# An RWKV-6 layer followed by a SwiGLU block: the same 1063 steps emitted in another order

## The chip, the cores and the metric

One core of a Trainium2 chip runs one launch of the kernel. The metric is device time in microseconds, the median of several executions. A profile of one execution goes with it; its times count from its own start.

## The reference

```python
# attention: B=4, H=8, S=768, D=48, float32
for t in range(S):
    cur = einsum('bhd,bhe->bhde', u * k[t], v[t])
    y[t] = einsum('bhd,bhde->bhe', r[t], state + cur)
    state = w[t][..., None] * state + einsum('bhd,bhe->bhde', k[t], v[t])
x = y as (B*S, H*D) = (3072, 384)
# feed-forward, d_ff = 1536
xn = x / sqrt(mean(x*x) + 1e-6) * rms_g
out = (silu(xn @ w_gate) * (xn @ w_val)) @ w_out
```

## The kernel before

The sequence is cut into six stages `n` of 128 tokens. A stage does this for its four batch entries `j`, and a step is named `function.n.j`. In the feed-forward part the second number of `gate_mm`, `val_mm`, `silu` and `h_mul` is `f`, one of 12 slices of d_ff, and covers all four batch entries (512 tokens).

The chunked recurrence for one (n, j) is this chain: `load_w` (SP), `ln` (ACT), `cs_mm` (PE: running sums of log w, into a ps_a and, in stages 0 to 2, a ps_b bank; `cs_add` on DVE makes the second one in stages 3 to 5), `exp_r` and `exp_k` (ACT), `r_mul` and `k_mul` (DVE: the scaled r and k, from `load_r` and `load_k`), their transpose, `q_mm` (PE, two ps_q banks), the masks `q_mask_e` (DVE) and `q_copy_o` with `q_mask_o` (ACT, then GpSimd; in stage 0 `q_mask_o` is on DVE and there is no copy), `y_mm` (PE). The transpose is `rk_pe` (PE) and a copy `rk_tr` (ACT) in stages 0 and 1, and a transposing DMA `rk_tr` on SP's queue from stage 2 on. The bonus term goes through `bonus_mul` (GpSimd, two instructions), `bonus_sum` (DVE) and `bonus_v` (GpSimd, from `load_v`). `cast_v` makes v bf16 (ACT in stages 0 and 1, GpSimd later). `st_mm` (PE) and `st_new` (DVE) carry the state to the next stage; `w_tot` (DVE) copies the decay of the chunk.

Then come `x_add` (DVE), `x_sq` (ACT), `x_rstd` (ACT in stage 0, GpSimd later), `xn_mul` (ACT), a transpose (`xn_pe` on PE and `xn_out` on DVE in stages 0 to 3; `xn_tr` by DMA on SP's queue and `xn_gain` on DVE in stages 4 and 5), and the feed-forward part: `gate_mm` (PE, three matmuls of 128x512 into a ps_a bank), `silu` (ACT), `val_mm` (PE, into a ps_b bank), `h_mul` (DVE, into a slice of the tile ht), `o_mm` (PE, 12 matmuls of 128x384, one for each f), `o_out` (ACT or DVE), `out_dma` (SP). The feed-forward of stage n is emitted among the recurrence of stage n+1. In the last stage `o_mm.5.3` and `o_mm.5.4` are the two halves of one batch entry.

The order of work is written out by hand in a string, `ORDER`. Each step is called once in that order:

```python
    for step in ORDER.split():
        fn, n, j = step.split(".")
        fns[fn](int(n), int(j))
```

Every engine runs its own instructions strictly in this order, SP's DMA queue included. What counts is therefore the order of the steps that share an engine. A step that waits holds back all that stand behind it on its engine, not the other engines. Tiles come from pools of fixed size: ps_a and ps_b have two banks each, ps_q four, inputs eight buffers for each of r, k, v and four for pairs of w, silu outputs three. The next allocation waits until a former holder has been read for the last time. The loads of one (n, j) are 192 KB each, with rows of 192 bytes.

The gate and value weights (`load_gv`, in a part for f below 4 and one for the rest) and the output weights (`load_wo`, three parts) go through GpSimd's queue, behind the GpSimd steps that are emitted ahead of them. `ln`, `exp_r`, `exp_k` and stage 0's `x_rstd` use one ACT table set, `silu` another:

```python
    def act(table_name, **kw):
        if table[0] != table_name:
            nc.scalar.preload_act_table_set(table_name)
            table[0] = table_name
        return nc.scalar.activation(**kw).ins
```

Each change between them in emission order loads a table.

Of the kernel before, what the change touches and what calls it, by code (L numbers as in the profile page):

```python
# [25 lines left out]
load_w.0.0 load_v.0.0 load_w.0.1 load_k.0.0 load_r.0.0 ln.0.0 load_w.0.2 load_r.0.1 ln.0.1 cs_mm.0.0 load_k.0.1  # L26
cs_mm.0.1 exp_k.0.0 load_w.0.3 exp_r.0.0 k_mul.0.0 bonus_mul.0.0 exp_r.0.1 r_mul.0.0 exp_k.0.1 load_r.0.2 w_tot.0.0
cast_v.0.0 rk_pe.0.0 ln.0.2 load_k.0.2 st_mm.0.0 r_mul.0.1 rk_tr.0.0 cs_mm.0.2 load_w.1.0 st_new.0.0 bonus_mul.0.1
q_mm.0.0 k_mul.0.1 load_v.0.1 w_tot.0.1 bonus_sum.0.0 ln.0.3 rk_pe.0.1 exp_k.0.2 q_mask_e.0.0 load_k.0.3 exp_r.0.2
cs_mm.0.3 q_mask_o.0.0 bonus_v.0.0 rk_tr.0.1 load_r.0.3 y_mm.0.0 k_mul.0.2 bonus_mul.0.2 exp_k.0.3 q_mm.0.1 load_w.1.1  # L30
r_mul.0.2 exp_r.0.3 x_add.0.0 ln.1.0 rk_pe.0.2 load_v.0.2 bonus_sum.0.1 x_sq.0.0 q_mask_e.0.1 cast_v.0.1 bonus_v.0.1
load_v.0.3 w_tot.0.2 rk_tr.0.2 q_mask_o.0.1 cs_mm.1.0 k_mul.0.3 load_w.1.2 q_mm.0.2 bonus_sum.0.2 bonus_mul.0.3
r_mul.0.3 load_k.1.0 q_mask_o.0.2 ln.1.1 rk_pe.0.3 x_rstd.0.0 load_w.1.3 cast_v.0.2 y_mm.0.1 bonus_v.0.2 rk_tr.0.3
load_r.1.0 x_add.0.1 load_gv.0.0 q_mask_e.0.2 cast_v.0.3 load_r.1.1 xn_mul.0.0 bonus_sum.0.3 load_gv.0.1 q_mm.0.3
ln.1.2 y_mm.0.2 bonus_v.0.3 x_sq.0.1 q_mask_e.0.3 st_mm.0.1 exp_k.1.0 w_tot.0.3 x_add.0.2 load_gv.1.1 cs_mm.1.1
x_rstd.0.1 q_mask_o.0.3 exp_r.1.0 load_gv.1.0 x_sq.0.2 y_mm.0.3 exp_k.1.1 xn_pe.0.0 x_add.0.3 st_mm.0.2 x_rstd.0.2
st_new.0.1 xn_mul.0.1 x_sq.0.3 st_new.0.2 st_mm.0.3 load_v.1.0 cs_mm.1.2 x_rstd.0.3 xn_out.0.0 xn_mul.0.2 xn_pe.0.1
# [643 lines left out]
```

## Time and profile before

| | |
|---|---|
| time, median of 3 runs | 207.25 us (207.13 to 207.8) |
| profiled execution, span from first to last instruction | 206.0 us |
| PE / DVE / ACT / GpSimd busy | 190.5 / 159.0 / 138.4 / 108.4 us |
| DMA | 32.41 MB, 157 GB/s on the mean |
| ACT table loads | 10, of 1283 ns |
| first `gate_mm` starts | 29.28 us |
| `o_mm.0.0` starts | 53.45 us |
| `o_mm.4.0` starts | 172.7 us |

The profiled execution's own time is known only as its span, 206.0 us; the timed median lies 1.25 us above it. The page gives busy time for each engine. PE's busy time has pipelined matmuls in it, so that a stretch can read as full at half the rate of another one; the spacing of the matmuls' starts tells the rate. In rows of the timeline the first number is the start, the second the duration of the row (with "xN", of N instructions together), and brackets give the idle time ahead and what ended it.

### The profile page before, as it was taken

To read this page: it belongs to the slowest core of one execution; us is meant where nothing else is said; L and a number is where in the kernel's file an instruction comes from. 1 tells how busy PE (TensorE), PEld (TensorE's weight loads), DVE (VectorE), ACT (ScalarE), POOL (GpSimd) and SP (SyncE) were. 2 spreads that over 40 slices of the span, in tenths; PEclk is the share of its full clock that TensorE was granted. 3 is DMA by queue.
4 is the path that set the end of the run, shared out by engine and by line. 5 is a ranking of instruction groups with operands and counts; after the bars stand their busy time and mean duration, and the time that the engine had idled before them with its cause. 6 is when DMAs were issued, how large, how long until landed. Compare 5 with 4: busy or idle time off the path is not lost.

```text
span 206.0 us, 4352 instructions
## 1 busy us (share of the span) xinstructions
PE 190.5 (92%) x1507; PEld 111.9 (54%) x1524; DVE 159.0 (77%) x323; ACT 138.4 (67%) x282; POOL 108.4 (53%) x167
## 2 busy tenths in 40 slices
PE   4695869899899999999999999999999999999993
PEld 2353534465665555765556565556555555555563
DVE  6398854799999899999999989899997855146311
ACT  3776994778987646989537978759978962334300
POOL 3398603399679668992699957948505510000000
PEclk9999999999999999999999999999999999999999
DMA  5999999999999899999899889796166110201032
GB/s 118 213 203 201 182 200 202 215 163 222 181 219 215 164 210 230 194 234 201 174 201 223 199 192 203 164 236 144 38 161 199 40 38 3 76 0 40 0 119 76
DMA packets 125727, 32.41 MB, mean 157 GB/s; under 512 B 120580, under 2 KB 124552, under 8 KB 125704
## 3 DMA queue, kind: packets, MB, share of 16 engines
q1 hardware_dynamic: 123664, 28.58, 66.8%
q0 software_dynamic: 2032, 3.54, 9.5%
q8 instruction: 12, 0.20, 0.4%
q14 instruction: 11, 0.09, 0.1%
q10 hardware_dynamic: 8, 0.00, 0.0%
HBM read 25.96 MB, written 4.72 MB: 149 GB/s over the span
## 4 chain that ended last, share of the span: by engine, by line
PE 69%; SPq 18%; DMA 5%; ACT 2%; POOL 2%; issue 1%; DVE 1%; ACTq 0%; DVEq 0%; POOLq 0%
PE ps_q L629 21%; PE ps_a L566 19%; PE ps_b L566 19%; SPq L211 15%; SPq L228 3%; DMA wo_sb<-in_moe_w_out_dram 3%; PE ps_q L458 2%; DMA rt<-in_r_dram 2%; PE ps_q L503 2%; PE ps_q L506 2%; PE ps_a L378 1%; PE ps_q L486 1%; PE ps_q L540 1%; POOL ruk L423 1%; PE ps_a L381 1%
## 5 line engine op out<-in xcount | busy, mean ns | idle before, releaser
L584 DVE TENSOR_TENSOR ht<-ps_b,sg 128x512 bf16<-128x512 f32 x72 | 49.0, 688 | 20.9 <-PE ps_b L566 14.5
L198 ACT ACTIVATE sg<-ps_a 128x512 bf16<-128x512 f32 x72 | 42.9, 598 | 32.6 <-PE ps_a L566 30.6
L566 PE MATMUL ps_a<-xnt,wg_sb 128*128 128x512 bf16 x207 | 59.3, 386 | 1.3 <-DMA wg_sb<-in_moe_w_gate_dram 0.5
L566 PE MATMUL ps_b<-xnt,wv_sb 128*128 128x512 bf16 x208 | 58.6, 384 | 0.3
L629 PE MATMUL ps_q<-wo_sb,ht 128*128 128x384 bf16 (+1 forms) x300 | 50.1, 319 | 0.3 <-DMA wo_sb<-in_moe_w_out_dram 0.3
L629 PEld LDWEIGHTS <-ht 128*128 128x128 bf16 x300 | 27.9, 97 | 16.8 <-DMA wo_sb<-in_moe_w_out_dram 0.5
L423 POOL TENSOR_TENSOR ruk<-rt,kt 128x384 f32<-128x384 f32 x24 | 24.6, 1024 | 22.6 <-DMA rt<-in_r_dram 15.4
L566 PEld LDWEIGHTS <-wv_sb 128*128 128x128 bf16 x216 | 23.6, 115 | 20.8 <-issue 2.1
L566 PEld LDWEIGHTS <-wg_sb 128*128 128x128 bf16 x216 | 23.4, 115 | 20.8 <-issue 1.3
L424 POOL TENSOR_TENSOR ruk<-ruk,u_bc 128x384 f32<-128x384 f32 x24 | 23.9, 997 | 1.9
L476 POOL TENSOR_SCALAR_AFFINE_SELECT qts<-qts 128x512 bf16<-128x512 bf16 x20 | 13.0, 650 | 14.4 <-ACT qts L469 14.4
L433 POOL TENSOR_TENSOR ydiag<-vt,diag 128x384 f32<-128x384 f32 x24 | 19.8, 830 | 0.0
L465 DVE TENSOR_TENSOR qts<-ps_q,mask_lt 128x512 bf16<-128x512 f32 x24 | 16.4, 683 | 2.1 <-PE ps_q L460 1.7
L529 ACT ACTIVATE xn<-xb,rstd 128x384 bf16<-128x384 f32 x24 | 14.4, 608 | 2.0 <-POOL rstd L525 1.9
L198 ACT ACTIVATE lw<-wt 128x384 bf16<-128x384 f32 x24 | 12.1, 516 | 4.8 <-DMA wt<-in_w_dram 4.6
L511 DVE TENSOR_TENSOR xb<-ps_q,ydiag 128x384 f32<-128x384 f32 x24 | 13.2, 551 | 2.0 <-PE ps_q L506 1.9
L469 ACT CAST qts<-ps_q 128x512 bf16<-128x512 f32 x20 | 11.6, 582 | 4.5 <-PE ps_q L460 4.5
L196 ACT ACT_TABLE_LOAD x10 | 12.8, 1283 | 1.8 <-PEq L665 1.6
L636 DVE COPY ob<-ps_q 128x384 f32<-128x384 f32 (+1 forms) x13 | 7.0, 539 | 8.7 <-PE ps_q L629 8.7
L516 ACT ACTIVATE junk<-xb 128x384 bf16<-128x384 f32 x24 | 12.5, 519 | 1.9 <-DVE xb L511 1.5
L428 DVE TENSOR_REDUCE diag<-ruk 128x8 f32<-128x384 f32 x24 | 12.9, 544 | 0.0
L417 DVE TENSOR_TENSOR rk<-kt,ps_b 128x384 bf16<-128x384 f32 x20 | 11.0, 548 | 2.4 <-DMA kt<-in_k_dram 1.9
(71 smaller groups left out, 269.6 us busy)
## 6 DMA issues: line engine op xcount, KB each, us to landing
wt<-in_w_dram SPq DMA_DIRECT2D x24, 192.0 KB, 3.9
vt<-in_v_dram SPq DMA_DIRECT2D x24, 192.0 KB, 3.8
kt<-in_k_dram SPq DMA_DIRECT2D x24, 192.0 KB, 3.8
rt<-in_r_dram SPq DMA_DIRECT2D x24, 192.0 KB, 3.9
out_dram<-ob SPq DMA_DIRECT2D x23, 192.0 KB, 2.2
wo_sb<-in_moe_w_out_dram POOLq DMA_DIRECT2D x3, 384.0 KB, 6.3
wv_sb<-in_moe_w_val_dram POOLq DMA_DIRECT2D x1, 768.0 KB, 10.7
wg_sb<-in_moe_w_gate_dram POOLq DMA_DIRECT2D x1, 768.0 KB, 14.2
```

Source lines behind the costliest of these rows:

```text
L198: return nc.scalar.activation(**kw).ins
L211: dmas["load_" + which, n, j] = nc.sync.dma_start(out=inp[which, n, j], in_=t[j, :, n * L:(n + 1) * L, :].rearrange("h t d -> t h d")).ins
L423: nc.gpsimd.tensor_tensor(out=ruk[n, j], in0=inp["r", n, j], in1=inp["k", n, j], op=ALU.mult)
L424: nc.gpsimd.tensor_tensor(out=ruk[n, j], in0=ruk[n, j], in1=u_bc, op=ALU.mult)
L433: nc.gpsimd.tensor_tensor(out=ydiag[n, j], in0=inp["v", n, j], in1=diag[n, j].to_broadcast([128, H, D]), op=ALU.mult)
L465: nc.vector.tensor_tensor(out=qts[n, j][:, 0], in0=bank["q", n, j][0], in1=bc_mid(mask_lt, NP), op=ALU.mult)
L476: nc.gpsimd.affine_select(out=qts[n, j][:, 1], in_=qts[n, j][:, 1], compare_op=ALU.is_gt, fill=0.0, base=0, pattern=[[0, NP], [1, 128]], c ...
L511: nc.vector.tensor_tensor(out=xb[n, j], in0=bank.pop(("y", n, j)), in1=ydiag[n, j].rearrange("p h d -> p (h d)"), op=ALU.add)
L529: nc.scalar.activation(out=xn, in_=xb[n, j], func=AF.Copy, scale=rstd[n, j][:, 1:2])
L566: nc.tensor.matmul(ps, lhsT=units(ws, c, f), rhs=xnt[n][:, c, :], start=(c == 0), stop=(c == KC - 1))
L584: nc.vector.tensor_tensor(out=ht[n][:, f, :], in0=bank.pop(("v", n, f)), in1=bank.pop(("sg", n, f)), op=ALU.mult)
L629: nc.tensor.matmul(ps[:, cols], lhsT=ht[n][:, f, b * L:(b + 1) * L], rhs=wo_sb[:, f, cols], start=(f == 0), stop=(f == FC - 1))
```

## The change

The string `ORDER` is replaced. It holds the same 1063 steps, each once; no function and no constant changes. The steps keep their engines. All six stages are reordered, the f slices of the feed-forward among them. The places that the prediction speaks of:

```diff
 ORDER = """
-load_w.0.0 load_v.0.0 load_w.0.1 load_k.0.0 load_r.0.0 ln.0.0 load_w.0.2 load_r.0.1 ln.0.1 cs_mm.0.0 load_k.0.1
-cs_mm.0.1 exp_k.0.0 load_w.0.3 exp_r.0.0 k_mul.0.0 bonus_mul.0.0 exp_r.0.1 r_mul.0.0 exp_k.0.1 load_r.0.2 w_tot.0.0
-cast_v.0.0 rk_pe.0.0 ln.0.2 load_k.0.2 st_mm.0.0 r_mul.0.1 rk_tr.0.0 cs_mm.0.2 load_w.1.0 st_new.0.0 bonus_mul.0.1
-q_mm.0.0 k_mul.0.1 load_v.0.1 w_tot.0.1 bonus_sum.0.0 ln.0.3 rk_pe.0.1 exp_k.0.2 q_mask_e.0.0 load_k.0.3 exp_r.0.2
...
-x_rstd.0.1 q_mask_o.0.3 exp_r.1.0 load_gv.1.0 x_sq.0.2 y_mm.0.3 exp_k.1.1 xn_pe.0.0 x_add.0.3 st_mm.0.2 x_rstd.0.2
-st_new.0.1 xn_mul.0.1 x_sq.0.3 st_new.0.2 st_mm.0.3 load_v.1.0 cs_mm.1.2 x_rstd.0.3 xn_out.0.0 xn_mul.0.2 xn_pe.0.1
-xn_mul.0.3 xn_out.0.1 xn_pe.0.2 ln.1.3 xn_pe.0.3 xn_out.0.2 exp_r.1.1 xn_out.0.3 exp_k.1.2 cs_mm.1.3 k_mul.1.0
-exp_r.1.2 gate_mm.0.0 st_new.0.3 exp_k.1.3 exp_r.1.3 val_mm.0.0 silu.0.0 gate_mm.0.1 h_mul.0.0 val_mm.0.1 silu.0.1
...
+load_w.0.0 load_w.0.1 load_r.0.1 load_r.0.0 ln.0.1 cs_mm.0.1 exp_r.0.1 ln.0.0 cs_mm.0.0 exp_r.0.0 r_mul.0.0 load_k.0.0
+bonus_mul.0.0 exp_k.0.0 k_mul.0.0 w_tot.0.0 load_w.0.2 rk_pe.0.0 r_mul.0.1 rk_tr.0.0 q_mm.0.0 load_w.0.3 load_k.0.1
+bonus_mul.0.1 bonus_sum.0.0 w_tot.0.1 exp_k.0.1 ln.0.2 k_mul.0.1 q_mask_o.0.0 cs_mm.0.2 load_v.0.0 ln.0.3 load_k.0.2
+q_mask_e.0.0 exp_k.0.2 k_mul.0.2 cs_mm.0.3 cast_v.0.0 rk_pe.0.1 exp_r.0.2 load_r.0.2 r_mul.0.2 load_v.0.1 bonus_v.0.0
+y_mm.0.0 rk_pe.0.2 rk_tr.0.1 q_mm.0.1 q_mask_e.0.1 q_mask_o.0.1 exp_r.0.3 load_r.0.3 load_w.1.0 cast_v.0.1 ln.1.0
+rk_tr.0.2 bonus_mul.0.2 bonus_sum.0.2 w_tot.0.2 load_v.0.2 cast_v.0.2 load_v.1.0 cast_v.1.0 load_w.1.3 bonus_sum.0.1
+bonus_v.0.1 w_tot.0.3 x_add.0.0 exp_k.0.3 x_sq.0.0 bonus_v.0.2 q_mm.0.2 y_mm.0.1 x_add.0.1 r_mul.0.3 x_sq.0.1
+x_rstd.0.1 load_k.0.3 k_mul.0.3 bonus_mul.0.3 st_mm.0.0 rk_pe.0.3 q_mask_e.0.2 cs_mm.1.0 st_mm.0.2 q_mask_o.0.2
+x_rstd.0.0 xn_mul.0.1 ln.1.3 bonus_sum.0.3 st_new.0.0 rk_tr.0.3 load_gv.0.0 load_gv.0.1 load_k.1.0 load_w.1.1
+load_v.0.3 bonus_v.0.3 cast_v.0.3 exp_k.1.0 y_mm.0.2 x_add.0.2 x_sq.0.2 xn_mul.0.0 x_rstd.0.2 load_w.1.2 ln.1.2
+q_mm.0.3 q_mask_o.0.3 st_mm.0.1 st_new.0.1 q_mask_e.0.3 k_mul.1.0 y_mm.0.3 load_gv.1.0 exp_r.1.0 xn_mul.0.2 ln.1.1
+cs_mm.1.2 exp_k.1.2 x_add.0.3 x_sq.0.3 x_rstd.0.3 st_new.0.2 load_r.1.0 st_mm.1.0 xn_pe.0.1 xn_out.0.1 r_mul.1.0
+cs_mm.1.1 exp_k.1.1 xn_mul.0.3 exp_r.1.1 xn_pe.0.2 xn_pe.0.0 xn_out.0.2 xn_out.0.0 rk_pe.1.0 rk_tr.1.0 st_mm.0.3
+st_new.0.3 bonus_mul.1.0 bonus_sum.1.0 bonus_v.1.0 load_gv.1.1 cs_mm.1.3 exp_k.1.3 exp_r.1.3 exp_r.1.2 xn_pe.0.3
+xn_out.0.3 q_mm.1.0 q_mask_e.1.0 gate_mm.0.0 silu.0.0 q_copy_o.1.0 q_mask_o.1.0 gate_mm.0.3 silu.0.3 val_mm.0.3
+h_mul.0.3 val_mm.0.1 load_r.1.1 r_mul.1.1 load_k.1.1 bonus_mul.1.1 k_mul.1.1 st_new.1.0 bonus_sum.1.1 gate_mm.0.1
...
+load_r.5.1 load_v.3.3 load_w.5.2 rk_tr.3.3 out_dma.1.0 rk_tr.3.2 gate_mm.2.4 silu.2.4 q_mask_o.3.0 y_mm.3.0 gate_mm.2.2
+silu.2.2 gate_mm.2.3 silu.2.3 o_out.1.3 val_mm.2.3 bonus_mul.3.1 bonus_sum.3.1 gate_mm.2.0 q_mm.3.1 q_copy_o.3.1
+bonus_v.3.0 x_add.3.0 bonus_sum.3.3 x_sq.3.0 load_w.5.1 load_r.5.0 st_mm.3.2 load_v.5.3 h_mul.2.3 gate_mm.2.9 q_mm.3.2
...
+val_mm.2.2 h_mul.2.2 gate_mm.2.5 silu.2.5 q_mask_e.3.1 val_mm.2.6 h_mul.2.6 st_mm.3.1 st_new.3.1 load_w.4.0 ln.4.0
+q_mask_e.3.2 x_rstd.3.0 cast_v.3.3 gate_mm.2.7 silu.2.7 val_mm.2.5 val_mm.2.9 h_mul.2.9 st_mm.3.3 gate_mm.2.8 silu.2.8
...
+q_mask_o.5.3 y_mm.5.3 bonus_v.5.3 x_add.5.3 x_sq.5.3 xn_mul.5.1 xn_tr.5.1 gate_mm.4.11 silu.4.11 val_mm.4.6 h_mul.4.6
+val_mm.4.11 h_mul.4.11 o_mm.4.1 o_mm.4.0 o_mm.4.3 x_rstd.5.3 xn_mul.5.3 xn_tr.5.3 xn_gain.5.2 out_dma.3.0 xn_gain.5.1
+xn_gain.5.0 val_mm.5.0 gate_mm.5.0 silu.5.0 gate_mm.5.1 o_out.4.0 val_mm.5.1 silu.5.1 h_mul.5.1 h_mul.5.0 o_mm.4.2
...
+h_mul.5.5 o_out.4.2 gate_mm.5.10 o_out.4.1 out_dma.4.1 val_mm.5.11 val_mm.5.10 silu.5.10 h_mul.5.10 silu.5.11
+h_mul.5.11 o_out.4.3 out_dma.4.3 out_dma.4.0 out_dma.4.2 o_mm.5.1 o_out.5.1 out_dma.5.1 o_mm.5.3 o_out.5.3 out_dma.5.3
+o_mm.5.2 o_out.5.2 out_dma.5.2 o_mm.5.0 o_out.5.0 out_dma.5.0 o_mm.5.4 o_out.5.4 out_dma.5.4
 """
```

## The prediction

> **What bounds the kernel now.** I read the page first, then busy time by stretch, then the PE, DVE, ACT and SP rows of the first 37 us, and the chain of waits.
>
> ```profile
> span 206.0 us, 4352 instructions
> ...
> PE 190.5 (92%) x1507; PEld 111.9 (54%) x1524; DVE 159.0 (77%) x323; ACT 138.4 (67%) x282; POOL 108.4 (53%) x167
> ...
> DMA  5999999999999899999899889796166110201032
> ```
>
> ```profile
> 0.00:29.30 29.30, 20.09 (x177) 12.53 (x178) 21.29 (x48) 21.91 (x51) 16.20 (x28) 1.00 1.00 185
> 29.30:53.40 24.10, 22.79 (x172) 12.31 (x173) 18.23 (x35) 17.38 (x28) 13.64 (x16) 1.00 1.09 203
> 53.40:143.00 89.60, 88.51 (x763) 52.94 (x773) 84.81 (x178) 67.31 (x142) 68.41 (x105) 1.00 0.99 201
> ```
>
> The second fence is busy time by stretch (PE, weight loads, DVE, ACT, POOL, granted clock, DMA share, GB/s). From 53.4 to 143 us PE works 88.5 of 89.6 us, DVE 84.8, and the DMA engines are full. An order can only lose there. The head (0 to 29.3 us, until the first `gate_mm`) is where nothing is full but the DMA.
>
> To place the losses I price PE's steps at their spacing in the dense stretch: `gate_mm` and `val_mm` 0.648 us each (144), `o_mm` 1.95 (23, and two halves of 0.99), `q_mm` 0.33 (24), `y_mm` 0.375 (20; 0.65 for the four of stage 0), `cs_mm` 0.70 (12) or 0.28 (12), `rk_pe` 0.45 (8), `st_mm` 0.17 (20), `xn_pe` 0.17 (16). The sum is 179.5 us of the 206.0. The 26.5 that are left lie as follows: 12.7 us of steps stand ahead of the first gate, which starts at 29.28, so 16.6 are lost there; from there to `o_mm.0.0` at 53.45 it takes 24.2 for 20.4, so 3.7; to `o_mm.4.0` at 172.7 it takes 119.3 for 116.2, so 3.1; the end after PE's last matmul is 3.2.
>
> ```profile
> 12.46 0.70 SPq L211 DMA_DIRECT2D kt<-in_k_dram  x1
> ...
> 15.22 1.94 SPq L211 DMA_DIRECT2D vt<-in_v_dram  x2
> 17.20 0.70 SPq L228 DMA_DIRECT2D wt<-in_w_dram  x1
> ```
>
> ```profile
> 16.50 0.55 DVE L417 TENSOR_TENSOR rk<-kt,ps_b 128x384 bf16<-128x384 f32 x1
> ...
> 23.58 0.56 DVE L511 TENSOR_TENSOR xb<-ps_q,ydiag 128x384 f32<-128x384 f32 x1 [0.62 <-PE ps_q L506]
> ```
>
> ```profile
> 29.28 0.59 PE L566 MATMUL ps_a<-xnt,wg_sb 128*128 128x512 bf16 x1
> 30.09 0.63 PE L566 MATMUL ps_a<-xnt,wg_sb 128*128 128x512 bf16 x1 [0.22 <-issue]
> 30.51 1.48 PE L566 MATMUL ps_b<-xnt,wv_sb 128*128 128x512 bf16 x3
> 31.79 1.48 PE L566 MATMUL ps_a<-xnt,wg_sb 128*128 128x512 bf16 x3
> 33.07 0.96 PE L566 MATMUL ps_b<-xnt,wv_sb 128*128 128x512 bf16 x3
> 33.87 0.81 PE L566 MATMUL ps_a<-xnt,wg_sb 128*128 128x512 bf16 x3
> 34.52 0.81 PE L566 MATMUL ps_b<-xnt,wv_sb 128*128 128x512 bf16 x3
> ```
>
> These are SP's loads, DVE's steps and PE's matmuls in order of time. `load_k.0.3` is the 14th load, issued at 12.46; `k_mul.0.3` follows at 16.50, `x_add.0.3` at 23.58, the first gate at 29.28. The last fence shows PE's rate: three 128x512 matmuls start 1.28 us apart until 33 us and 0.65 apart after that. PE runs at half rate through the head and its first four MoE groups, although the granted clock reads 1.00 throughout. 29.28 to 33.87 holds 4.59 us for 2.59 of work, so 2.0 of the 3.7 lost in that stretch are this.
>
> **The change part by part.** No step is added or removed; every instruction keeps its engine. So the sum is PE's losses, stretch by stretch.
>
> *The head.* On SP, `load_k.0.3` moves from 14th to 18th: `load_r.0.3`, `load_v.0.2`, `load_v.1.0` and `load_w.1.3` now go ahead of it. The 18th load of before was issued at about 16.2 (second of the x2 row at 15.22), and the page gives 3.8 to 3.9 us to landing, so it lands near 20.2 instead of 16.3. At 197 KB each and the 200 GB/s of that stretch four loads are 3.9 us. Followed through the new queues, with durations from the rows: DVE does `x_add.0.1` and `r_mul.0.3` first, `k_mul.0.3` runs 21.0 to 21.5; `rk_pe.0.3` 1.03 to 22.6; `rk_tr.0.3` on ACT behind `ln.1.3`, 1.0, to 24.0; `q_mm.0.3` behind `y_mm.0.2`, to 25.1; on DVE `q_mask_o.0.3` 0.68, `st_new.0.1` 0.72 and `q_mask_e.0.3` 0.68, to 27.0; `y_mm.0.3` 0.7, `x_add.0.3` 0.55, to 28.3; on ACT `exp_k.1.2` 0.5, `x_sq` 0.7, `x_rstd` 0.5, `exp_k.1.1` (it waits for `cs_mm.1.1` behind two other PE steps) and `xn_mul.0.3` 0.6, to 31.3; then `exp_r.1.1` 0.4, `rk_tr.1.0` 1.0, `exp_k.1.3` and `exp_r.1.3` 0.5 each, which wait on `cs_mm.1.3`, to 34.0. Only `exp_r.1.3` frees one of the two ps_a banks, so `gate_mm.0.0` starts at 34.0 against 29.3. From `k_mul.0.3` to the gate this is 13.0 us, before 12.8: the shift is that of the load. Ahead of the gate PE now also does `st_mm.1.0`, `rk_pe.1.0` and `q_mm.1.0`, 13.6 us of steps instead of 12.7. Lost: 20.4 instead of 16.6.
>
> The bounds: with no queueing at all, landing to gate is k_mul 0.55, rk_pe 1.03, rk_tr 1.0, q_mm 0.6, two masks 1.36, y_mm 0.65, x_add 0.55, x_sq 0.7, x_rstd 0.5, xn_mul 0.6, xn_pe 0.4, xn_out 0.55, with some 0.9 of hand-overs 9.4 us, so the gate at 29.6. From above: `bonus_sum.1.0` now stands ahead of `xn_out.0.3` on DVE and needs `load_r.1.0`. In the run of before that load came in at 31.5 (POOL waited 7.4 us), behind the gate weights: between 28 and 35 us the weights' queue moved 1.29 MB and the loads' 0.12. Now the weights are issued at about 22.9 (after `bonus_mul.0.3`) instead of 19.96, and the 23rd load is due at about 25, just ahead of them. Were it caught, 31.5 + 2.07 + 0.54 + 0.55 + 0.1 puts the gate at 34.8. I take 34.0, near the upper end, since ACT has work queued for all of 16 to 34 us.
>
> *First MoE stage.* Before lost 3.7 here: 2.0 at half rate, 0.7 waiting at `gate_mm.0.4` for weights, the rest in small waits. The new order pays the half rate again, about 2.3 with the small ones. The weights of `val_mm` for f of 4 and more are now issued behind `bonus_v.1.0`, at 34.2; with 768 KB behind the others at the 0.18 MB/us of before they land at 41 to 45, and `val_mm.0.4` comes 11.5 us after the gate, at 45.6: hidden, 0 to 1 us if not. `load_wo` is issued at 43.6 to 46 us (41.8 to 47.3 before) and needed at 55.5: hidden. Lost up to `o_mm.0.0`: 20.4 + 2.3 = 22.7 against 20.3, so +2.4.
>
> On the half rate: before, PE was busy 20.1 of 29.3 us with waits between and stayed slow until it had worked without a gap from 28.5 to 33. In my account PE is without gaps from 27 to 34, ahead of the gate. [...]
>
> *The dense stages (53 to 203 us).* I compared each PE step's cover (PE work between the step that feeds a chain and the one that needs it) with the chain's own durations, with up to three queue neighbours in between. The old order has no uncovered site from stage 1 on; the new one has `o_mm.2.0`, `o_mm.3.0`, `o_mm.4.1` and `o_mm.5.1` directly behind the `val_mm` that ends their `h_mul` (0.5, 0.7, 0.7, 1.4 us). Each needs that slice of ht only at its 11th or 12th matmul, 1.6 to 1.8 us in: 0, or 3.3 if it waits for the whole tile. `ln.4.0` now stands among the silus of stage 2, so there are 12 table loads instead of 10, 1.28 us each, on an ACT that is 67% busy: `silu.2.7` ends some 13.5 us after the stage's first gate, and `gate_mm.2.11` needs its bank at 14.1. The cover is 0.6 us; beyond it, each microsecond costs one. `xn_tr.5.3` comes later, 6.3 us of chain (2.3 of it landing) under 7.8 us of `o_mm` and MoE: hidden. DVE's queue between the end of stage 0's `xn_out` and `xn_gain.4` is 111 us instead of 114, PE's 116 instead of 118: no new bound. I take 0 for this part, from -1.5 (half of the 3.1 lost there) to +3.
>
> Sum: 206.0 + 2.4 = 208.4 of span. The timed median is 207.25, 1.25 over the span of the profiled execution; so 209.6 us.
>
> **The rivals.** *The stage 4 load decides as well:* on SP, `load_r.5.1`, `load_w.5.2`, `load_w.5.1`, `load_r.5.0` and `load_v.5.3` now go ahead of `load_w.4.0`, with two transposes. I have it landing 10 us after the stage's first gate, with `ln.4.0` due at 11.1. Two us of further lateness hold `silu.2.7` behind `ln.4.0`, PE for 1.5, and the later loads of stages 3 and 4 with it: 212. For it: SP's rows there are nearly gapless, with transposes of 1.2 to 2.0 us. Against: the old order ran equally thin and PE waited 1.1 us in all after 53.4.
>
> *Faster:* one mechanism, a denser head. If ACT and DVE let the gate start by 32.5, and PE's unbroken work ahead of it has brought the full rate, the losses up to `o_mm.0.0` are 32.5 - 13.6 + 0.2 = 19.1 against 20.3: 206.0. It decides from a gate at 31.6 with the half rate, or at 33.9 with the full one. For it: three more PE steps are done ahead. Against: the four places of `load_k.0.3`.
>
> *No effect that can be told:* the extra steps and the rate just pay for the load: 207.2.
>
> **How the numbers follow.** Head late with the rest hidden: 0.46, with 208 to 211.3 for its own range (the dense part's ends and the gate 1.5 early or 0.8 late). Stage 4 loads too: 0.18. No effect: 0.12. Faster: 0.24. A measurement here tells about 0.3%, 0.6 us, from no change. Slower is 0.46 + 0.18 = 0.64. The range runs from 205.6 (the faster case, with some of the dense loss regained) to 213.3 (the stage 4 case and a microsecond).
>
> **What would show it.** `k_mul.0.3` near 21 and the first `gate_mm` near 34 us with 1.28 us groups behind it; `o_mm.0.0` near 55.5; PE 98% busy after that; 12 table loads with no PE wait at `gate_mm.2.11`. A first gate before 31.6, or groups of 0.65 from its start, would make me wrong towards faster; a PE wait of over 1 us after 56 us, towards slower.

## The result and the profile after

The new order takes 210.58 us (median of 4 runs, 210.02 to 210.94) against 207.22 (4 runs, 207.13 to 207.8) for the old one: a ratio of 1.0132, 95% interval 1.0092 to 1.0172. The profiled execution took 210.94 us and has a span of 208.9, against 206.0 before. The forecast of 209.6 was near, but as the last sections show, two of its terms were wrong by about two microseconds each, in opposite directions, so that it was near by luck.

The page of the new order, first its span, PE's busy time and the slices of granted clock and DMA share:

```profile
span 208.9 us, 4345 instructions
...
PE 188.9 (90%) x1524; PEld 111.2 (53%) x1524; DVE 160.3 (77%) x323; ACT 139.8 (67%) x284; POOL 108.8 (52%) x167
...
PEclk9997579999999999999999999999999999999999
DMA  7999999989869999799999989961467102200142
```

Busy time by stretch of the new order (columns as in the same view of before: PE, weight loads, DVE, ACT, POOL, granted clock, DMA share, GB/s):

```profile
0.00:29.30 29.30, 17.53 (x172) 12.01 (x173) 20.92 (x46) 21.24 (x50) 17.64 (x29) 0.83 1.00 188
29.30:53.40 24.10, 21.69 (x178) 12.11 (x176) 19.51 (x36) 17.29 (x31) 14.58 (x19) 1.00 1.08 203
53.40:143.00 89.60, 87.05 (x757) 50.95 (x754) 81.47 (x173) 67.99 (x138) 59.20 (x91) 1.00 0.97 192
```

In the long dense stretch PE is busy for 87.05 us instead of 88.51, and DVE for 81.47 instead of 84.81. In the first two stretches the DMA share is at 1.00 or over in both kernels; what follows from that row is taken up with e12_less.

The steps that the prediction followed, from DVE's, SP's and PE's timelines of the new order:

```profile
15.37 1.94 SPq L210 DMA_DIRECT2D kt<-in_k_dram  x2
```

```profile
18.05 0.47 ACT L197 ACTIVATE ps_b<-ps_b 128x384 f32<-128x384 f32 x1
```

```profile
19.10 0.56 DVE L510 TENSOR_TENSOR xb<-ps_q,ydiag 128x384 f32<-128x384 f32 x1 [0.41 <-POOL ydiag L432]
...
20.04 0.55 DVE L416 TENSOR_TENSOR rk<-kt,ps_b 128x384 bf16<-128x384 f32 x1
```

```profile
28.13 0.48 PE L383 MATMUL ps_b<-lw,mask_nle 128*128 128x384 bf16 x1
...
30.39 0.32 PE L383 MATMUL ps_b<-lw,mask_nle 128*128 128x384 bf16 x1
...
31.99 1.46 PE L565 MATMUL ps_a<-xnt,wg_sb 128*128 128x512 bf16 x6 [0.56 <-DVE xnt L550]
33.29 1.46 PE L565 MATMUL ps_b<-xnt,wv_sb 128*128 128x512 bf16 x6
```

`load_k.0.3` is issued at 15.37. `k_mul.0.3` runs at 20.04, not waiting for the load but standing behind `x_add.0.1`, which waited for GpSimd; on ACT its `exp_k.0.3` had come at 18.05, where the old order had it at 13.35. The same kind of `cs_mm` matmul takes 0.48 us at 28.13 and 0.32 at 30.39: the full rate comes at about 29 us, ahead of the first gate at 31.99, and six 128x512 matmuls then start within 1.3 us.

Where PE lost its time, with the prediction's prices for PE's steps (lost is the start of a step less the priced work ahead of it, in us):

| step | before: start, lost | after: start, lost | difference |
|---|---|---|---|
| `gate_mm.0.0` | 29.28, 16.6 | 31.99, 18.4 | +1.8 |
| `o_mm.0.0` | 53.45, 20.4 | 53.73, 21.0 | +0.6 |
| `q_mm.3.0` | 93.8, 20.4 | 96.1, 22.7 | +2.3 |
| `o_mm.2.0` | 114.1, 21.8 | 117.7, 24.5 | +2.7 |
| `o_mm.3.0` | 143.1, 22.1 | 146.7, 25.7 | +3.6 |
| `o_mm.4.0` | 172.7, 23.1 | 176.3, 26.0 | +2.9 |
| `o_mm.5.4` | 201.6, 23.1 | 204.5, 26.0 | +2.9 |

Of the 2.9 us, 2.3 come after `o_mm.0.0`, where the forecast had nothing. PE's chain of waits between 53 and 176 us, for the new order (us in total, times, longest):

```profile
PE ps_q L485 <- ACT ob L637: 1.0, 1, 1.0
PE ps_q L628 <- ACT ob L637: 0.6, 1, 0.6
PE ps_q L459 <- DVE xb L510: 0.4, 1, 0.4
```

and how the longest of them came about, in the timelines of SP, ACT and PE:

```profile
100.22 0.58 SPq L643 DMA_DIRECT2D out_dram<-ob  x1
```

```profile
103.17 0.48 ACT L637 COPY ob<-ps_q 128x384 f32<-128x384 f32 x1 [1.50 <-DMA out_dram<-ob]
```

```profile
103.70 0.33 PE L485 MATMUL ps_q<-vb,rk 128*128 128x96 bf16 x4 [1.03 <-ACT ob L637]
```

There are three output buffers. `out_dma.1.0` is issued on SP at 100.22; `o_out.1.3` on ACT waits for the buffer that this store reads until 103.17, 2.9 us after the issue, and the ps_q bank that it has to empty stays taken meanwhile; PE's `st_mm.3.2` waits for that bank.

### The profile page after: what moved, and what is told of

Read it like the earlier page. It is cut to its first block, busy times and chain, and to the rows that moved or that the text cites. A ratio compares the mean times of both kernels' runs of the same rounds, so it can differ in the third digit from the quotient of the medians.

```text
span 208.9 us, 4345 instructions
## 1 busy us (share of the span) xinstructions
PE 188.9 (90%) x1524; PEld 111.2 (53%) x1524; DVE 160.3 (77%) x323; ACT 139.8 (67%) x284; POOL 108.8 (52%) x167
## 4 chain that ended last, share of the span: by engine, by line
PE 59%; DVE 18%; ACT 8%; DMA 7%; issue 3%; SPq 2%; POOL 0%; DVEq 0%; ACTq 0%
PE ps_q L628 20%; PE ps_b L565 14%; PE ps_a L565 14%; DVE ht L583 5%; DMA wt<-in_w_dram 4%; DMA out_dram<-ob 3%; DVE st L493 3%; DVE qts L464 2%; DVE diag L427 2%; PE ps_a L377 2%; DVE ps_q L491 2%; PE ps_q L439 2%; PE ps_q L505 2%; PE ps_q L457 2%; ACT sg L197 1%
## 5 line engine op out<-in xcount | busy, mean ns | idle before, releaser
L583 DVE TENSOR_TENSOR ht<-ps_b,sg 128x512 bf16<-128x512 f32 x72 | 48.2, 686 | 23.6 <-PE ps_b L565 12.2
L197 ACT ACTIVATE sg<-ps_a 128x512 bf16<-128x512 f32 x72 | 42.3, 598 | 33.5 <-PE ps_a L565 23.3
L565 PE MATMUL ps_b<-xnt,wv_sb 128*128 128x512 bf16 x216 | 56.2, 380 | 1.1 <-DVE ht L583 0.8
L565 PE MATMUL ps_a<-xnt,wg_sb 128*128 128x512 bf16 x216 | 55.9, 380 | 0.6 <-DVE xnt L550 0.6
L628 PE MATMUL ps_q<-wo_sb,ht 128*128 128x384 bf16 (+1 forms) x300 | 49.6, 319 | 0.6 <-ACT ob L637 0.6
L628 PEld LDWEIGHTS <-ht 128*128 128x128 bf16 x300 | 28.4, 97 | 17.5 <-issue 0.7
L565 PEld LDWEIGHTS <-wv_sb 128*128 128x128 bf16 x216 | 23.0, 114 | 19.7 <-issue 1.8
L475 POOL TENSOR_SCALAR_AFFINE_SELECT qts<-qts 128x512 bf16<-128x512 bf16 x20 | 12.7, 642 | 16.7 <-ACT qts L468 16.7
L411 DVE TENSOR_TENSOR rk<-rt,ps_a 128x384 bf16<-128x384 f32 x20 | 10.9, 547 | 3.9 <-ACT ps_a L197 3.6
L197 ACT ACTIVATE ps_a<-ps_a 128x388 f32<-128x388 f32 x20 | 9.5, 481 | 5.1 <-DVE ps_b L388 2.6
L457 PE MATMUL ps_q<-rkT 48*128 48x128 bf16 x96 | 9.7, 226 | 3.5 <-ACT rkT L448 3.4
```

The lines of the kernel that those rows point to most:

```text
L457: nc.tensor.matmul(qe[:, i, :], lhsT=t[0:D, NP + i, :], rhs=t[0:D, i, :], start=(i == 0), stop=(i == NP - 1))
L565: nc.tensor.matmul(ps, lhsT=units(ws, c, f), rhs=xnt[n][:, c, :], start=(c == 0), stop=(c == KC - 1))
L583: nc.vector.tensor_tensor(out=ht[n][:, f, :], in0=bank.pop(("v", n, f)), in1=bank.pop(("sg", n, f)), op=ALU.mult)
L628: nc.tensor.matmul(ps[:, cols], lhsT=ht[n][:, f, b * L:(b + 1) * L], rhs=wo_sb[:, f, cols], start=(f == 0), stop=(f == FC - 1))
```

## Experiments

Twelve kernels were run, each beside the old order on the same chip; ratios are against that. One table for all (us, by the same prices; the dense loss is counted from `o_mm.0.3`, behind the seams of the spliced orders, to `o_mm.4.0`):

| kernel | first gate: start, lost | `o_mm.0.0`: start, lost | dense loss | ratio, 95% interval |
|---|---|---|---|---|
| old order | 29.3, 16.6 | 53.5, 20.4 | 3.27 | |
| new order | 32.0, 18.4 | 53.7, 21.0 | 5.76 | 1.0132 (1.0092 to 1.0172) |
| e1_old_head | 29.3, 16.7 | 60.9, 28.2 | 6.60 | 1.0526 (1.0465 to 1.0587) |
| e2_new_head | 32.0, 18.4 | 55.8, 22.7 | 3.27 | 1.0155 (1.0094 to 1.0217) |
| e3_out_dma | 32.6, 19.0 | 54.4, 21.7 | 5.56 | 1.0111 (1.0035 to 1.0187) |
| e4_load_k | 32.7, 19.1 | 54.8, 22.1 | 4.64 | 1.0190 (1.0125 to 1.0255) |
| e5_ob4 | 32.4, 18.8 | 53.6, 20.8 | 5.15 | 1.0164 (1.0117 to 1.0210) |
| e6_warm | 29.0, 16.3 | 56.3, 23.2 | 3.27 | 0.9983 (0.9949 to 1.0017) |
| e7_gv | 32.8, 19.2 | 54.7, 21.6 | 3.27 | 1.0025 (0.9990 to 1.0061) |
| e8_head | 33.4, 19.9 | 55.1, 22.3 | 5.28 | 1.0152 (1.0098 to 1.0205) |
| e9_split | 29.1, 16.5 | 55.1, 22.0 | 3.26 | 1.0006 (0.9976 to 1.0036) |
| e10_warm_split | 30.3, 17.6 | 55.2, 22.1 | 3.99 | 1.0012 (0.9978 to 1.0046) |
| e11_new_moe0 | 32.3, 18.7 | 56.3, 22.8 | 3.26 | 1.0116 (1.0051 to 1.0182) |
| e12_less | 29.2, 16.5 | 50.9, 17.8 | 4.54 | 0.9917 (0.9885 to 0.9949) |

The starts and losses are those of one execution each, on several chips: there the old order took 208.1 to 209.6 us in the median, against 207.2 in the result. Five executions with the new order's head start their first gate between 32.0 and 32.6, and e9_split, as fast as the old order beside it, starts `o_mm.0.0` 1.6 us later than the old order's trace. Smaller differences than these say nothing by themselves; the ratios are measured side by side.

### What makes the head late: e4_load_k, e8_head

The first puts back the load on which the forecast's head rests:

```diff
-exp_r.0.3 load_r.0.3 ... x_rstd.0.1 load_k.0.3 k_mul.0.3
+exp_r.0.3 load_k.0.3 load_r.0.3 ... x_rstd.0.1 k_mul.0.3
```

> New order with load_k.0.3 back near its old place on SP (13th instead of 18th). The prediction's step says the head is late by this load: then k_mul.0.3 and the first gate come 3 us earlier or more and the time falls by 1 to 2 us. The rival from the new trace: k_mul.0.3 at 20.04 has no idle time ahead of it, its DVE queue (x_add.0.1, which waits for bonus_v.0.1 on GpSimd, then r_mul.0.3) sets it; then the gate moves by less than 0.5 us and the time by less than 0.3.

SP and DVE of this kernel:

```profile
11.06 0.88 SPq L211 DMA_DIRECT2D kt<-in_k_dram  x1
```

```profile
20.31 0.55 DVE L417 TENSOR_TENSOR rk<-kt,ps_b 128x384 bf16<-128x384 f32 x1
```

The load goes 4.3 us earlier and `k_mul.0.3` does not: 20.31 against 20.04. The first gate is at 32.7, no earlier. The lateness of the head is not this load's.

The second moves that chain's steps forward on ACT, DVE and PE too:

```diff
-exp_r.0.3 ... rk_tr.0.2 ... exp_k.0.3 x_sq.0.0 ... r_mul.0.3 ... k_mul.0.3 ... rk_pe.0.3 ... rk_tr.0.3 ... st_new.0.1 q_mask_e.0.3
+exp_r.0.3 exp_k.0.3 ... rk_tr.0.2 r_mul.0.3 k_mul.0.3 rk_pe.0.3 ... rk_tr.0.3 x_sq.0.0 ... q_mask_e.0.3 ... st_new.0.1
```

> The new order with load_k.0.3 ahead of load_r.0.3 as in the run before, and with the third batch entry's chain moved forward on its engines as well: exp_k.0.3 directly behind exp_r.0.3 on ACT, r_mul.0.3, k_mul.0.3 and rk_pe.0.3 directly behind rk_tr.0.2, rk_tr.0.3 ahead of x_sq.0.0, q_mask_e.0.3 behind q_mask_o.0.3 and ahead of st_new.0.1. Theory A (ACT's and DVE's queue positions set the head's lateness): k_mul.0.3 starts at 16.5 to 18 instead of 20.0, the first gate at 30 to 31 instead of 32.0, and the time falls by 0.5 to 2 us, to 208.6 to 210.1. Theory B (the chains of the other batch entries and of stage 1, which stand ahead of the gate, are as long): k_mul.0.3 is early but the gate still starts at 31.7 or later, and the time stays at 210.3 or more.

`k_mul.0.3` starts at 17.64, 2.4 us earlier, and `rk_tr.0.3` at 19.13 instead of 22.18. Then the gain is gone: `q_mm.0.3` runs at 22.55 (23.22 in the new order), `x_add.0.3` at 27.71 (26.59) and the first gate at 33.4. So one chain brought forward pushes the others back, and the gate does not come with it. What both orders share is a full ACT. Between 18 and 29.3 us, in the old order and then in the new one:

```profile
18.00:29.30 11.30, 8.27 (x83) 5.44 (x84) 8.55 (x19) 10.66 (x30) 6.01 (x8) 1.00 1.08 185
18.00:29.30 11.30, 7.37 (x83) 5.41 (x80) 10.29 (x23) 10.34 (x31) 9.07 (x10) 0.55 1.03 183
```

ACT is busy for 10.66 and 10.34 of 11.30 us; in the new order DVE is as full (10.29, against 8.55). The new order places three more ACT steps ahead of `xn_mul.0.3` (`cast_v.1.0`, `ln.1.3`, `exp_k.1.2`; 40 instead of 37), and ACT has been busy for 21.0 instead of 19.8 us when it comes. That would be 1.3 of the gate's 2.7. It is read from the traces and not shown: no kernel here took those three steps away, and DVE's fuller queue is an untested rival.

### Where the dense loss belongs: e1_old_head, e2_new_head, e11_new_moe0

Three splices. The first has the old order up to `val_mm.0.3`, and then what is left in the new order:

```diff
-ORDER = new order
+ORDER = old order ahead of load_k.1.1, then all other steps in the new order
```

> Old order up to val_mm.0.3, then every other step in the new order. The new order's trace puts its extra PE loss at +1.8 us at the first gate, +0.6 us at o_mm.0.0 and +2.3 us between o_mm.0.0 and o_mm.4.0. If the dense stages carry the loss (theory D), this kernel keeps it: 0.6 us under the new order or less, 209.5 to 210.6 us, with the first gate near 29.3. If the head carries it (the place named in the prediction), it comes down to 207 to 208 us.

It reaches the first gate at 29.3, as the old order does, and `o_mm.0.0` at 60.9, because the new order's rest wants stage 1's v, r and k early and the old head has queued them behind the weights: PE waits 3.5 us for `cast_v.1.0` and 1.1 for `rk_tr.1.0`. Head and rest of an order fit one another; a splice pays at the seam.

The second has the new head, the third the new order as far as `o_mm.0.0`:

```diff
-ORDER = new order
+ORDER = new order ahead of gate_mm.0.0, then all other steps in the old order    # e2_new_head
+ORDER = new order ahead of o_mm.0.0, then all other steps in the old order       # e11_new_moe0
```

> New order for all steps that it emits ahead of gate_mm.0.0, then every other step in the old order: the other half of the exchange. Theory D: 207.2 to 208.2 us, first gate near 32 us and, as in the new order, at full rate from its first matmul. The head as the cause: 209 to 211 us.

> All steps that the new order emits ahead of o_mm.0.0, in its order; the others in the old order. Of the 3.3 us that the new order is slower, 0.6 had come about by o_mm.0.0 and 2.3 between o_mm.0.0 and o_mm.4.0. Theory A (the dense part's loss is made by the order of the later stages): o_mm.0.0 has lost 21 to 21.7 as in the new order, from there to o_mm.4.0 the loss is 2.7 to 3.1 as in the old one, the time is 0.6 to 1.6 over the old order. Theory B (the loss is left over from the first stage, which ends with DVE, GpSimd and the loads further behind): from o_mm.0.0 to o_mm.4.0 4.4 to 5.1 are lost again, and the time is 2.5 to 3.5 over the old order.

Both pay at the seam as well: e2_new_head 3.0 us at `val_mm.0.4` for the value weights, e11_new_moe0 1.8 at `cs_mm.2.0` and 1.5 at `cs_mm.2.1`, which is why its time missed the expected 0.6 to 1.6 us over the old order. Behind the seam the traces agree. The old order's dense part costs 3.26 or 3.27 us in six kernels with different starts (the old order itself, e2_new_head, e6_warm, e7_gv, e9_split, e11_new_moe0); only e10_warm_split and e12_less have more, with waits of their own in stages 1 and 2. The new order's costs 4.6 to 5.8 in five (the new order itself, e3_out_dma, e4_load_k, e5_ob4, e8_head), and more in e1_old_head. The dense loss is made by the order of the later stages, not left over from the first. In the time itself e7_gv shows it, further down: the new head with the old order behind it, and one weight issue moved, takes the old order's time within 0.6%.

### Whether the output buffers make it: e3_out_dma, e5_ob4

Both take away the two waits shown above, one by moving three stores forward on SP, one by a fourth buffer with no step moved:

```diff
+... out_dma.0.0 load_w.3.0 ... out_dma.0.3 load_k.3.0 ... out_dma.1.0 rk_tr.3.0 ...      # e3_out_dma
```

```diff
-ob = pt.tile([128, DM], FP32, name="ob", bufs=3)
+ob = pt.tile([128, DM], FP32, name="ob", bufs=4)      # e5_ob4
```

> New order with three output transfers moved forward on SP alone: out_dma.0.0 ahead of load_w.3.0, out_dma.0.3 ahead of load_k.3.0, out_dma.1.0 ahead of rk_tr.3.0. Theory D names them: o_out.1.1 and o_out.1.3 on ACT wait for one of the three ob buffers, hold a ps_q bank, and PE waits 0.6 us at o_mm.1.3 and 1.0 us at st_mm.3.2. If so, both waits go and the time falls by 1.6 us, to about 209.0. If DVE, 91% busy there, is the real limit of the stage, the waits go and PE loses the same elsewhere: 210.0 to 210.9.

> The new order with four instead of three output buffers (ob); no step is moved. In the run of the new order o_out.1.1 and o_out.1.3 wait on ACT for a buffer whose out_dma is late on SP, and PE loses 0.75 and 1.1 us behind them; from o_mm.0.0 to o_mm.4.0 the new order loses 5.05 us where the old one loses 2.72. Theory A (the buffers are the cause): both waits go, the dense part loses 3.0 to 3.5 us, the time falls by 1.5 to 1.9 to about 208.9. Theory B (the buffers hide another lateness, as when the three out_dma were moved forward on SP and 4.85 us were lost in other places): both waits go, other waits come in their place, the dense part still loses 4.5 or more, the time stays within 0.5 us of 210.6.

PE's waits between 53 and 176 us in the kernel with four buffers:

```profile
PE ps_a L566 <- ACT sg L198: 0.4, 1, 0.4
PE ps_q L460 <- DVE xb L511: 0.4, 1, 0.4
PE ps_q L458 <- DMA rkT<-rk: 0.4, 1, 0.4
PE ps_b L566 <- DVE ht L584: 0.3, 1, 0.3
```

Both waits for `ob` are gone in both kernels. Of the 1.85 us that PE lost behind them by the prices, the dense part gets back 0.2 and 0.6; the rest appears as waits of 0.3 to 0.6 us for ACT, DVE and a transposing DMA. Neither ratio lies below the new order's by more than its interval, and that of e5_ob4 rules out the expected 1.5 to 1.9 us. Two kernels of the first part show it without any such step: e4_load_k and e8_head have three buffers and the stores in their places, and lose 0.0 and 0.15 us at these two steps in their executions; they still lose 4.6 and 5.3 us in the dense part and are 1.9 and 1.5% slower than the old order. So the waits were real in the new order's execution and are not what makes the order slow.

What repeats is smaller. In all six kernels with the new dense order PE loses, by the prices, 0.3 us at `cs_mm.2.3`, 0.3 to 0.4 at `val_mm.1.7`, 0.3 to 0.75 at `cs_mm.3.2` and 0.5 in `q_mm.4.2` (the wait for `xb` above), 1.3 to 1.8 together; none of the others loses over 0.1 at any of them. The old dense order loses 0.55 at `cs_mm.4.0` and 0.52 at `cs_mm.5.1`, in every kernel that has it, and the new one nothing there. The new order's further losses fall in other places from one execution to the next. Which of its moves make them was not settled.

### What the full rate is worth, and what bounds the first stage: e6_warm, e7_gv, e9_split, e10_warm_split, e12_less

The old order's half rate was priced at 2.0 us. The next kernel fills PE's gaps ahead of the first gate with repeats of transposes that PE does anyway:

```diff
-for c in range(KC):
+for c in list(range(KC)) * {(0, 1): 5, (0, 3): 2}.get((n, j), 1):     # in xn_pe
     nc.tensor.transpose(ps[:, c, :], xn[:, c * 128:(c + 1) * 128], ident)
```

> The old order, with the three transposes of xn_pe.0.1 done five times over and those of xn_pe.0.3 twice, into the same PSUM tile: 15 matmuls of 128x128 that change no value and fill PE's idle 1.07 us at 26.1 and 0.29 us at 28.2, so that PE works without a gap from 25.65 us to the first gate at 29.28. Theory A (the full rate comes after about 3.3 us without a gap, as in the new order between 25.98 and 29.3): the first gate starts at 29.2 to 29.5 and its groups are 0.65 us apart instead of 1.28 from the start; of the 2.0 us paid there 1.5 to 2.0 come back; time 205.3 to 205.8. Theory B (the rate depends on more than gaps, or these matmuls are too small to count): groups stay 1.28 us apart until about 33 us, and the time is 207.2 to 207.6. Theory C: the rate comes, but the first gate group then waits for weights or for exp_k.1.3 and exp_r.1.3 on ACT, which free its PSUM banks, and half of the gain goes: 206.2 to 206.6.

Its PE rows, and its waits between 28 and 56 us:

```profile
25.36 2.87 PE L540 MATMUL ps_q<-ident,xn 128*128 128x128 bf16 x24 [0.16 <-ACT xn L529]
28.23 0.32 PE L378 MATMUL ps_a<-lw,mask_lt 128*128 128x384 bf16 x1
...
28.98 0.81 PE L566 MATMUL ps_a<-xnt,wg_sb 128*128 128x512 bf16 x3 [0.17 <-ACT er L198]
```

```profile
PE ps_a L566 <- DMA wg_sb<-in_moe_w_gate_dram: 3.7, 1, 3.7
```

The full rate is there at 28.2, the first gate runs at it, four gate and value groups are done by 34.6 instead of 36.5, and the time is the same (0.9983, 0.9949 to 1.0017). PE now waits 3.7 us for the gate weights of f 4 and more, where the old order waited 0.7. The profiled execution of this kernel, 210.76 us, is the slowest of its twelve and its weights land some 1.3 us later than the old order's, so a usual wait is nearer 2.4 us (an estimate). The unchanged median fits a gain that goes into this wait; its interval leaves room for 1 us of gain and not for the 2.0.

In e7_gv the second value weights of e2_new_head are issued earlier, at 25.27 instead of 32.15 us:

```diff
-load_gv.1.0 ... bonus_mul.1.0 bonus_sum.1.0 bonus_v.1.0 load_gv.1.1
+load_gv.1.0 load_gv.1.1 ... bonus_mul.1.0 bonus_sum.1.0 bonus_v.1.0
```

> The kernel with the new head and the old order from gate_mm.0.0 on, with one step moved: load_gv.1.1 (the value weights for f of 4 and more) directly behind load_gv.1.0 on GpSimd's queue, ahead of bonus_mul.1.0 and bonus_v.1.0, which wait there 3.9 us for load_r.1.0 and its sum. It is then issued at about 25.2 instead of 32.2 us. Theory A (the 3.1 us wait of val_mm.0.4 was this issue's place): the wait goes, o_mm.0.0 has lost 19.5 to 20 instead of 22.7, time 207.0 to 208.2, at the level of the old order. Theory B (the weights only share the DMA engines with the loads): load_r.1.0 and load_k.1.0 land later, bonus_sum.1.0 holds xn_out.0.3, the first gate moves from 32.0 to 33 or later, and the time is 209 to 210.5.

The wait of 3.0 us shrinks to 1.7, not to nothing, and the first gate starts at 32.8 instead of 32.0. The issue is 6.9 us earlier, but the landing takes 15.2 us instead of 8.8, so the weights come only 0.5 us sooner, which fits DMA engines that are full there (a share of 1.12 to 1.22 in every microsecond from 25 to 34). The rest of the shorter wait is the later gate. Even so `o_mm.0.0` has lost 21.6 instead of 22.7 us, and the ratio is 1.0025 (0.9990 to 1.0061), where e2_new_head has 1.0155: the time, though not the wait, came out as theory A had it. The new head with the old order behind it costs no more than 0.6%, so most of the new order's 1.3% belongs to what stands behind the head.

In e9_split and e10_warm_split the second part of the weights is cut in two, in the second one with the repeats:

```diff
-GV = (0, 4, 12)
+GV = (0, 4, 8, 12)
-... load_gv.1.1 ... load_gv.1.0 ...
+... load_gv.1.0 load_gv.1.1 ... load_gv.2.0 load_gv.2.1 ...
```

> The old order with the second part of the gate and value weights (768 KB each, f of 4 to 11) cut in two: GV = (0, 4, 8, 12), so that the weights of f 4 to 7 (384 KB each) are issued on GpSimd at 22.55 and 23.35 us and those of f 8 to 11 behind them. No other step is moved. PE still reaches its first gate at 29.3 at half rate. Theory A (in the old order the half rate is paid in full, 2.0 us, and the weights only cost the 0.66 us wait at gate_mm.0.4): the wait goes, o_mm.0.0 has lost 19.7, the time falls by 0.6 to 0.7. Theory B (the weights of f 8 to 11 land no earlier than 38 to 39 us and the wait only moves from gate_mm.0.4 to gate_mm.0.8): no change that can be told. Theory C (the smaller packets are slower to move): the wait grows, 0.5 to 1 us slower.

> The same three weight parts, with the repeated transposes of xn_pe.0.1 (five times) and xn_pe.0.3 (twice) that bring the full rate ahead of the first gate. With the repeats alone PE did its first four MoE groups from 29.0 to 34.6 us at full rate and then waited 3.7 us for the second gate weights, which had landed at 38.9; the time did not change. Theory A (the half rate was hidden: the second weights set the pace of the first MoE stage, and a warm PE only waits for them; with those of f 4 to 7 there by 34.5 us both gains come through): no wait over 0.5 us at gate_mm.0.4 and gate_mm.0.8, o_mm.0.0 has lost 17.7 to 18.5 instead of 20.4, the time falls by 2 to 2.6 us against the old order. Theory B (all weights together are late, whatever their parts): the wait of 3.7 us moves or shrinks by under 1 us, and the time stays within 0.7 us of the old order.

Neither moves the time. PE's waits between 28 and 56 us in e9_split, then in e10_warm_split:

```profile
PE ps_q L440 <- DVE rk L412: 1.3, 1, 1.3
PE ps_q L629 <- DMA wo_sb<-in_moe_w_out_dram: 0.8, 1, 0.8
```

```profile
PE ps_q L440 <- DVE rk L417: 1.4, 1, 1.4
PE ps_q L629 <- DMA wo_sb<-in_moe_w_out_dram: 0.5, 1, 0.5
```

The wait for weights is gone, and in its place stand waits for `r_mul.1.2` and `k_mul.1.1`, and for the output weights. What those two wait for is seen on DVE, again in e9_split and then in e10_warm_split:

```profile
44.63 0.56 DVE L412 TENSOR_TENSOR rk<-rt,er 128x384 bf16<-128x384 f32 x1 [0.96 <-DMA rt<-in_r_dram]
```

```profile
41.50 0.56 DVE L417 TENSOR_TENSOR rk<-kt,ek 128x384 bf16<-128x384 f32 x1 [1.57 <-DMA kt<-in_k_dram]
```

Stage 1's loads land behind the weights. In the old order, between 28 and 35 us, the two queues moved as many packets (660 for the weights, 653 for the loads, whose rows have 192 bytes), but 1.29 MB against 0.12 MB:

```profile
q0 software_dynamic: 660, 1.29, 96.8%
q1 hardware_dynamic: 653, 0.12, 16.1%
```

(In e10_warm_split the first gate group still ran at half rate, 1.23 us from 30.29 to 31.52; the full one came during the first value group, which took 0.80, and the next took 0.64.) The waits change names, and `o_mm.0.0` stays between 53.5 and 56.3 us in all kernels so far but e1_old_head. By 53 us the old order has moved 10.21 MB (193 GB/s) and the new one 10.35 MB (195 GB/s). The last kernel takes bytes away:

```diff
 def load(which, n, j):
+    if n == 1 and j > 0:
+        inp[which, n, j] = inp[which, n, 0]
+        return
```

> The kernel with three weight parts and the repeated transposes, with nine loads of 192 KB left out: stage 1's r, k and v are loaded for batch entry 0 alone and its tiles stand in for entries 1 to 3, so stage 1 computes with the wrong r, k and v there; every other instruction remains. With all loads, full rate and early weights had moved the loss from one wait to the next (weights, then stage 1's k and r, then the output weights), and o_mm.0.0 stayed at 53 to 56 us, with the DMA engines full from 18 us on. Theory A (what must be brought in ahead of o_mm.0.0, about 10.3 MB at some 195 GB/s or 53 us, sets its start in all these kernels): with 1.77 MB less, 9 us of transfer, no wait for r, k or output weights is left there, o_mm.0.0 starts at 50.5 to 52.5 instead of 55.2 and has lost 17.5 to 19.5 instead of 22.1, and the time falls 2 to 3.5 us below that of the old order. Theory B (DVE's, ACT's and GpSimd's queues hold the stage up, the loads are hidden anyway): o_mm.0.0 stays at 54.5 or later, the time within 0.7 us of the old order's.

Busy time by stretch and PE's waits (20 to 60 us) in that kernel:

```profile
29.30:53.50 24.20, 23.46 (x194) 13.64 (x196) 21.63 (x40) 19.08 (x34) 15.80 (x20) 1.00 1.06 189
```

```profile
PE ps_q L462 <- ACT rkT L453: 1.1, 1, 1.1
PE ps_q L544 <- ACT xn L533: 0.6, 1, 0.6
PE ps_q L490 <- ACT vb L341: 0.3, 1, 0.3
```

No wait for a DMA is left on PE, and PE is busy for 23.46 of 24.20 us. `o_mm.0.0` starts at 50.9, 2.5 us ahead of the earliest of the others, and the time falls below the old order's, the only time that does so by more than its interval (0.9917, 0.9885 to 0.9949), although 1.3 us of it are given back later. So behind the old order's head the loads set the pace up to `o_mm.0.0`: a faster PE (e6_warm) or weights in smaller parts (e9_split, e10_warm_split) moved the waits and not the time, and fewer loads moved the time. Two things are not separated. The DMA share is still 1.06, and by 53 us 9.90 MB had moved against 10.21 in the old order, so the loads of later stages took the room, and the nine loads left out also free nine places in SP's queue. And this kernel has the full rate from its first gate (0.65 us from 29.17 to the value group at 29.82), which e10_warm_split reached only in the first value group. It leaves needed work out and is no version to keep. None of those that compute everything is shown to beat the old order.

For the new order the same was not shown. PE's waits between 28 us and `o_mm.0.0` there, in which no DMA stands:

```profile
PE ps_b L565 <- DVE ht L583: 0.8, 1, 0.8
PE ps_a L565 <- DVE xnt L550: 0.6, 1, 0.6
PE ps_q L439 <- DVE rk L416: 0.5, 1, 0.5
```

The longest is that of `val_mm.0.2` for the bank that `h_mul.0.1` empties, and DVE had `r_mul.1.1`, `k_mul.1.1`, `st_new.1.0` and `bonus_sum.1.1` to do first, none of which waited for a load. The last output weights landed at 52.96, 0.8 us ahead of `o_mm.0.0`: close, but PE did not wait for them.

## Why the prediction was right, and where it was not

*Head, +3.8 forecast, +1.8 measured.* `k_mul.0.3` was put at 21.0 and ran at 20.04, but the reason given, the place of `load_k.0.3` on SP, falls with e4_load_k. From `k_mul.0.3` to the gate it took 12.0 us instead of the 13.0 of the account, so the gate came at 31.99 and not 34.0. The step that failed is the first: the chain was followed from the load, where ACT's and DVE's queues already held the step back. Nor does the gate follow the chain: e8_head starts `k_mul.0.3` 2.4 us earlier, and the gate comes at 33.4. What does make the gate late stays open; ACT's three further steps are a reading.

*First MoE stage, the half rate paid again: wrong.* The groups run 0.65 us apart from the start. The account had PE without gaps ahead of the gate and priced the half rate into the first groups all the same. In the trace PE has no wait from 25.98 to 30.1 us, and the full rate is there at 29.04, where eight 128x128 transposes take 0.61 us instead of the 1.07 at 20.18. Yet from the gate to `o_mm.0.0` 2.5 us are lost by the prices, against the 2.3 of the forecast (3.7 in the old order): the term came out right by luck, with waits for DVE where the half rate was put. The faster rival took the 2.0 us away and put nothing in their place. What the rate itself is worth was measured in the old order alone, where e6_warm leaves at most 1 us.

*Up to `o_mm.0.0`, +2.4 forecast, +0.6 measured.* The forecast is +3.8 at the gate and -1.4 behind it, the measurement +1.8 and -1.2. So the term that was mis-sized is the gate's, by 2.0 us. The forecast also read the row that the DMA engines were full in the head and made no term of it; e12_less shows that the loads count in the old order, and in the new one no wait for a DMA was seen on PE in that stretch.

*Dense stages, 0 forecast (from -1.5 to +3), +2.3 measured.* This is the mis-sized term that carries the result. The comparison of covers named four sites and priced each at 0, and was right on each: `o_mm.2.0`, `o_mm.3.0`, `o_mm.4.1` and `o_mm.5.1` have no wait for `ht`; the 12 table loads, 1.28 us each, cost nothing (lost is 24.5 at `gate_mm.2.11` and still at `o_mm.2.0`); `xn_tr.5.3` is hidden (lost is 26.0 at `o_mm.4.0` and still at `o_mm.5.4`). What it did not have is waits at other places: in this execution 1.85 us behind the output buffers, a resource that passes from stage to stage through SP, and 1.3 at the four places that lose in every kernel with this dense order; on the other side, the old order's 1.1 us at `cs_mm.4.0` and `cs_mm.5.1` went away. By the experiments the 1.85 us are not the cause: without them other places lose nearly as much. Which moves do it stays open. "PE 98% busy" was 97% (87.05 of 89.60), and one per cent of that stretch is 0.9 us. (The old order's own loss there, put at 3.1, is 2.7 by the table.)

*The sum.* 208.4 us of span was forecast and 208.9 measured, with 1.8 too much in front and 2.3 too little behind. In the profiled execution the part around the span was 2.04 us; the 1.25 of the forecast set a median against the span of another execution. The number was near by luck: slower was right, and the place named for it, the head, was not where most of it arose.

*The rivals.* Of the stage 4 load nothing is seen: `load_w.4.0` is issued 10.8 us later than before, and PE loses 0.2 us between `o_mm.2.0` and `q_mm.4.0`. The faster case had its conditions fulfilled, gate by 32.5 and full rate, and still did not come: it put 0.2 us of loss between the gate and `o_mm.0.0`, where 2.5 were lost in waits for DVE above all, and nothing behind. By the forecast's own signs, "groups of 0.65 from its start" spoke for faster and "a PE wait of over 1 us after 56 us" for slower; only the second was a sign of the time.

## What to carry to other kernels

Before a stretch's losses are priced by an engine's waits, set the bytes that must have come by its end against the rate of the row: where the engines that move them are full (a DMA share of 1.06 and more here), a faster rate or smaller parts may only change what is waited for, as in e6_warm, e9_split and e10_warm_split. In a dense stretch count the resources that go from stage to stage (buffers and the queue that frees them) beside the chains, and take "no uncovered site found" as a bound on what was looked at, not as zero. A wait that a trace names is shown to be the cause only when the time comes back with it; here two waits went and the loss stayed. And look for the same wait in a second execution of the same order before mending it: these two were absent from two others.

## What the hardware showed

The rate of PE and the granted clock of the rows do not always agree. In the old order the clock reads 1.00 throughout while 128x512 matmuls start 0.43 us apart until 33 us. In the new order it reads 0.50 from 24 to 29 us, yet the same kind of `cs_mm` matmul takes as long in both (0.48 us at 28.13 in the rows above, and in the old order):

```profile
28.94 0.48 PE L384 MATMUL ps_b<-lw,mask_nle 128*128 128x384 bf16 x1
```

In these traces the spacing is the surer reading. Nor did the full rate come after a fixed time without a gap: 2.9 us or less in e6_warm (from 25.36 to 28.23, after a gap of only 0.16), about 3.1 in the new order (from 25.98 to 29.04), and over 4.4 in e10_warm_split (from 26.64 until after 31.1). What brings it is not shown by these runs.
